# Three edits to the planner of a fused attention and SoLU kernel: the load time of chunk 3, the place of the centring of w_out, and q @ kv joined to the next chunk's kv

## The chip, the cores and the metric

The kernel runs on one core of one Trainium2 chip. The metric is the device time of one execution in microseconds (us). The kernel before took 196.27 us as the median of four runs, which lie between 195.92 and 196.62 us. Reading a profile, this text calls the engines by their short names: PE is TensorE (matrix products), ACT is ScalarE, DVE is VectorE, POOL is GpSimd, and SP is the engine that mostly issues stores here.

## What is computed

Two stages follow each other. The first is an attention without softmax for 8 batches and 8 heads of 576 positions and 64 channels, normed by its root mean square over the channels:

```python
kv = np.einsum('bhsd,bhse->bhde', k, v)
out = np.einsum('bhsd,bhde->bhse', q, kv)
rms = np.sqrt(np.mean(out * out, axis=-1, keepdims=True) + 1e-06)
x = out / rms * g_norm          # then heads side by side: 4608 tokens x 512
```

The second takes these 4608 rows through an expansion to 1024 channels, the SoLU activation (h times its softmax), a layer norm over the 1024 channels and a projection back to 512:

```python
h = x @ w_in
e = np.exp(h - h.max(-1)); sm = e / (e.sum(-1) + 1e-09)
solu = h * sm
ln = (solu - mean) / np.sqrt(var + 1e-06) * g_ln
out = ln @ w_out
```

Inputs and output are float32; the kernel computes its products in bf16.

## The kernel before

**Chunks.** The tokens are worked through in nine chunks of 512. Chunk c, for c from 0 to 7, holds the first 512 positions of batch c. Chunk 8 holds the last 64 positions of all batches. For a chunk the steps are: load k, v and q, which POOL issues as casting transfers (`load_kv`, L208, and `load_q`, L217); kᵀv of all heads (`kv_mm`, L275), 72 small products into one bank named misc and, from chunk 2 on, one bank named s; six copies of it to bf16 (`kv_copy`, L294, half of them on DVE and half on ACT from chunk 2 on); q turned so that channels lie on the partitions (`qT_mm` and `qT_copy` on PE for chunks 0 to 3, a transposing transfer of SP for the later ones); q @ kv for the first and the second half of the heads (`o_mm`, L337), each into two banks, mostly those named o; for each of these banks a square on ACT, a mean over the channels on PE (`s_mm`, into the single bank s), a logarithm and an exponential on ACT, and a product on DVE that makes x (`x_mul`, L387).

Then for each f of eight slices of 128 expanded channels: `h_mm` (L468, four products into one of two banks named h), an exponential on ACT (`h_exp`), the product u on DVE (`h_u`), the square of u on ACT or POOL (`u_sq`, called usq here), and for each pair of slices a sum of two exponentials on POOL (`e_sum`, called es). `sums` (L528) adds u, usq and es over the channels on PE into the bank misc (of chunk 0: into a bank h). `stats` on DVE and `rstd` on ACT turn these into one factor per token. `out_mm` (L581) is the projection, as two groups of four products for each of four blocks of 128 tokens, into one of two banks named out. `scale` (L612) multiplies a block by its factor on DVE, which frees the bank, and SP stores it.

The division by the sum of exponentials cancels in the layer norm, but for the constant that is added to the variance. The mean is taken out ahead of the projection: `w_mean` (L567) computes the weighted mean of the rows of w_out on PE into a bank out, and eight instructions of DVE, `w_center` (L575), write the centred, scaled bf16 weights that every `out_mm` reads. The bank of the mean is free again only after the last of them.

**The planner.** No order is written out. `Plan` (L19) gets pieces: a name, an engine, an assumed length, a rank, the pieces that it needs, and the buffers that it begins or uses. `order` (L33) is a greedy list scheduler. It keeps a clock for each engine and takes, again and again, the piece that can start earliest; where several could start at the same time, the one of the lowest rank. It models when buffers come free, a change of TensorE's tile shape (0.1 us, L67), and the load queue (L71 to L74): a load adds its assumed time to the queue, and its data count as there 1.3 us later. The order so found is the program order of each engine. On the chip each engine executes its own instructions in that order and waits where a piece is not ready, whatever else could run. The assumed times therefore take no time themselves; they only decide who stands behind whom.

Three products matter for tile shape: `kv_mm` and `o_mm` run in tiles of 64x64, `sums` in tiles of 128x32, everything else on the full 128x128.

Of the kernel before, what the change touches and what calls it, by code (L numbers as in the profile page):

```python
# [18 lines left out]
class Plan:  # L19
# [3 lines left out]


    def __init__(self, bufs):
        self.pieces, self.users, self.bufs = {}, {}, bufs

    def add(self, name, engine, length, rank, fn, needs=(), uses=(), first=(), load=0.0):
        self.pieces[name] = (engine, length, rank, fn, needs, first, load)
        for key in (*uses, *first):  # L30
            self.users.setdefault(key, []).append(name)

    def order(self):  # L33
        free, done, queue, lanes, mode = {}, {}, 2.5, [], {}
        held = {tag: [] for tag in self.bufs}
        waiting = {n: set(p[4]) for n, p in self.pieces.items()}
        behind = {}
        for n, needs in waiting.items():
            for m in needs:
                behind.setdefault(m, []).append(n)  # L40
        ready = [n for n, needs in waiting.items() if not needs]
        order = []
        while ready:
            best = None
            for n in ready:
                engine, length, rank, fn, needs, first, load = self.pieces[n]
                t = max([free.get(engine, 0.0)] + [done[m] for m in needs])
                more = {}
                for key in first:
                    old = held[key[0]] + more.setdefault(key[0], [])  # L50
                    more[key[0]].append(key)
                    if len(old) >= self.bufs[key[0]]:
                        last = self.users[old[-self.bufs[key[0]]]]
                        t = max([t] + [done.get(m, 1e9) for m in last])
                if load and len(lanes) >= 8:
                    t = max(t, lanes[-8])
                if t < 1e8 and (best is None or (t, rank) < best[:2]):
                    best = (t, rank, n)
            t, rank, n = best
            engine, length, rank, fn, needs, first, load = self.pieces[n]  # L60
            ready.remove(n)
            for key in first:
                held[key[0]].append(key)
            if engine == "pe":

                tiling = n[0] if n[0] in ("kv_mm", "o_mm", "sums") else "full"
                length += 0.1 if mode.get(engine, tiling) != tiling else 0.0  # L67
                mode[engine] = tiling
            free[engine] = t + length
            done[n] = t + length + {"pe": 0.2, "sp": 2.5}.get(engine, 0.12) + (2.0 if n[0] == "qT" and engine == "sp" else 1.0 if n[0] == "gate" else 0.0)  # L70
            if load:  # L71
                queue = max(queue, t + length + 1.0) + load
                done[n] = queue + 1.3
                lanes.append(done[n])  # L74
            order.append(fn)
            for m in behind.get(n, ()):
                waiting[m].discard(n)
                if not waiting[m]:
                    ready.append(m)
        assert len(order) == len(self.pieces)  # L80
        return order
# [3 lines left out]
def kernel(  # L85
# [21 lines left out]
    B, H, S, D = q.shape  # L107
# [5 lines left out]
    NC = B + 1  # L113
# [7 lines left out]
    bufs = {  # L121
        "k": 3, "v": 3, "q": 3, "qT": 3, "osq": 4, "lss": 2, "rst": 2, "oc": 2, "x": 2, "e": 4, "u": 2, "usq": 2, "es": 2,
        "ob": 4,
    }
# [8 lines left out]
    plan = Plan({**banks, **bufs})  # L133
# [113 lines left out]
    for b in range(B):  # L247
        at = b - 9.0 if b > 1 else (-2.0, -1.5)[b]
        behind = [] if b < 2 else [("h_mm", 0, 0)] if b == 2 else ([("gate", b - 1)] if b - 1 in XBAR else []) + [("h_mm", b - 3, 2 if b == 3 else 0)]
        for g, hs in enumerate(heads(b)):  # L250
            part = 0.1 * g
            n = len(heads(b))
            for i, (name, src) in enumerate((("k", k), ("v", v))):
                plan.add((name, b, g), "pool", 0.75 if n == 1 else 0.6, at + part + 0.01 * i,
                         lambda name=name, src=src, b=b, hs=hs: load_kv(name, src, b, hs),
                         behind, uses=[(name, b)] if g else [],
                         first=[] if g else [(name, b)], load=2.9 / n if b < 4 else 3.5)
            plan.add(("q", b, g), "pool", 0.9 if n == 1 else 0.7, at + part + (0.02 if b < 2 else 0.1),
                     lambda b=b, hs=hs: load_q(b, hs), behind,
                     uses=[("q", b)] if g else [], first=[] if g else [("q", b)], load=2.7 / n if b < 4 else 3.3)  # L260
        plan.add(("q_last", b), "pool", 0.6, 2.0 + 0.5 * b, lambda b=b: load_q_last(b),
                 [("h_mm", 2 + b // 2, 4 * (b % 2))], load=0.5)
    for half in range(2):
# [133 lines left out]
    for c in range(NC):  # L397
# [4 lines left out]
        if c < B:  # L402
            for xs in ((0,), (1,)) if c < 2 else ((0, 1),):
                g = xs[0]
                rg = r + 0.5 * w * g
                plan.add(("kv_mm", c, g), "pe", 0.65, rg, lambda c=c, xs=xs: kv_mm(c, xs), [("k", c, g), ("v", c, g)],
                         uses=[("k", c), ("v", c)], first=[(kv_tag(c, x), "kv", c, x) for x in xs])
                for x in xs:
                    for part in range(3):
                        plan.add(("kv", c, x, part), kv_engine(c, x), 0.25, rg + 0.05,  # L410
                                 lambda c=c, x=x, part=part: kv_copy(c, x, part), [("kv_mm", c, g)],
                                 uses=[(kv_tag(c, x), "kv", c, x)])
        if c in XBAR:
            plan.add(("qT", c), "sp", 1.8, r - 0.1, lambda c=c: q_turn(c),
                     [("q", c, 0)] if c < B else [("q_last", b) for b in range(B)],
                     uses=[("q", c)] if c < B else [], first=[("qT", c)])
# [3 lines left out]
        for hf in range(2):  # L420
            g = group(c, hf)
            tag = ("out", "h")[c] if c < 2 and hf else "o"
            if c not in XBAR:
# [7 lines left out]
                         first=[] if hf else [("qT", c)])  # L431
# [3 lines left out]
                     uses=[("qT", c)], first=[(tag, c, hf, z) for z in range(2)])  # L435
            for z in range(2):
                i = (c, hf, z)
                rz = r + w * (0.4 + 0.5 * hf + 0.12 * z)
                if (c, hf) in COPIED and z:
                    plan.add(("oc", i), "dve", 0.62, rz, lambda i=i: o_copy(*i), [("o_mm", c, hf)],  # L440
                             uses=[(tag, *i)], first=[("oc", i)])
                    plan.add(("sq", i), "pool", 1.05, rz + 0.01, lambda i=i: o_sq_copy(*i), [("oc", i)],
                             uses=[("oc", i)], first=[("osq", i)])
                else:
                    plan.add(("sq", i), "act", 0.57, rz, lambda i=i: o_sq(*i), [("o_mm", c, hf)],
                             uses=[(tag, *i)], first=[("osq", i)])
                stag = "h" if i in ((0, 0, 1), (0, 1, 0)) else "s"
                plan.add(("s_mm", i), "pe", 0.22, rz + 0.02, lambda i=i, stag=stag: s_mm(i, stag), [("sq", i)],
                         uses=[("osq", i)], first=[(stag, i)])
                if c == 0:  # L450
                    plan.add(("ex", i), "act", 0.6, rz + 0.04, lambda i=i: s_rsqrt(*i), [("s_mm", i)],
                             uses=[(stag, i)], first=[("rst", i)])
                else:
                    plan.add(("ln", i), "act", 0.6, rz + 0.03, lambda i=i: s_ln(*i), [("s_mm", i), "table"],
                             uses=[(stag, i)], first=[("lss", i)])
                    plan.add(("ex", i), "act", 0.6, rz + 0.04, lambda i=i: s_exp(*i), [("ln", i)],
                             uses=[("lss", i)], first=[("rst", i)])
                plan.add(("x", i), "dve", 0.67, rz + 0.06, lambda i=i: x_mul(*i),
                         [("ex", i)] + ([("x", (c, 0, 0))] if (hf, z) != (0, 0) else []),
                         uses=[(tag, *i), ("rst", i)] + ([("x", c)] if (hf, z) != (0, 0) else []),  # L460
                         first=[("x", c)] if (hf, z) == (0, 0) else [])
# [44 lines left out]
    for c in range(NC):  # L506
        for f in range(NF):
            r = c + f / 8
            plan.add(("h_mm", c, f), "pe", 0.87, r, lambda c=c, f=f: h_mm(c, f),
                     [("w_in", f // 4), *[("x", (c, *i)) for i in xs]], uses=[("x", c)], first=[(h_bank(c, f), "h", c, f)])  # L510
            plan.add(("exp", c, f), "act", 0.57, r + 0.02, lambda c=c, f=f: h_exp(c, f),
                     [("h_mm", c, f), "table"] + ([("exp", c, f - 1)] if f % 2 else []), uses=[(h_bank(c, f), "h", c, f)] + ([("e", c, f // 2)] if f % 2 else []),
                     first=[] if f % 2 else [("e", c, f // 2)])
            plan.add(("u", c, f), "dve", 0.62, r + 0.04, lambda c=c, f=f: h_u(c, f),
                     [("exp", c, f)] + ([("u", c, 0)] if f else []), uses=[(h_bank(c, f), "h", c, f), ("e", c, f // 2)] + ([("u", c)] if f else []),
                     first=[] if f else [("u", c)])
            engine = "act" if f in {0: (2, 4, 6, 7), 1: (), NC - 1: (1, 3, 5, 6, 7)}.get(c, (2, 6)) else "pool"
            plan.add(("usq", c, f), engine, 0.57 if engine == "act" else 1.05, r + 0.15 if c else -0.6,
                     lambda c=c, f=f, engine=engine: u_sq(c, f, engine), [("u", c, f)] + ([("usq", c, 0)] if f else []),
                     uses=[("u", c)] + ([("usq", c)] if f else []), first=[] if f else [("usq", c)])  # L520
            if f % 2:
                n = f // 2
                plan.add(("es", c, n), "pool", 1.28, r + 0.1, lambda c=c, n=n: e_sum(c, n),
                         [("exp", c, f)] + ([("es", c, 0)] if n else []), uses=[("e", c, n)] + ([("es", c)] if n else []),
                         first=[] if n else [("es", c)])
# [49 lines left out]
    def w_center(f):  # L575
        nc.vector.scalar_tensor_tensor(
            out=w_out_sb[:, f, :], in0=w_out_f[:, f, :].bitcast(FP32), scalar=g_ln_sb[:, f:f + 1],
            in1=T["mean"][:, :], op0=MUL, op1=SUB,
        )
# [48 lines left out]
    plan.add("w_mean", "pe", 2.0, -0.5, lambda: [w_mean(f) for f in range(NF)], ["w_out", "g_mean", ("o_mm", 0, 1)],  # L628
             first=[("out", "mean")])
    for f in range(NF):  # L630
        plan.add(("w_center", f), "dve", 0.67, 0.05 + 0.12 * f, lambda f=f: w_center(f), ["w_mean"], uses=[("out", "mean")])
    for c in range(NC):
        r, rs = (c + 1, c + 1) if c else (0.55, -0.5)
        parts = [[("u", c, f) for f in range(NF)], [("usq", c, f) for f in range(NF)], [("es", c, n) for n in range(NF // 2)]]
# [13 lines left out]
        for m in range(3 if c == NC - 1 else 4):  # L648
            tag = "o" if c == NC - 1 and m > 1 else "out"
            for half in range(2):  # L650
# [7 lines left out]
            plan.add(("store", c, m), "act" if c == NC - 1 and m % 2 else "sp", 0.6, r + (2 * m + 3) / 8, lambda c=c, m=m: store(c, m),  # L658
                     [("ob", c, m)], uses=[("ob", c, m)])

    for fn in plan.order():
        fn()

# [29 lines left out]
```

## Time and profile before

| | |
|---|---|
| median of four runs | 196.27 us (195.92 to 196.62) |
| profiled execution, its own time | 196.05 us |
| span of the profiled execution, first to last instruction | 194.3 us |
| mean granted TensorE clock | 0.994 |
| PE busy | 178.9 us (92%) |
| ACT busy | 140.2 us (72%) |
| POOL busy | 129.6 us (67%) |
| DVE busy | 122.2 us (63%) |
| DMA queue of the loads (software dynamic) | 17.30 MB, 54.8% of 16 engines' span |

The span is what the profile's rows lie in; the execution's own time is longer by what happens ahead of the first and behind the last instruction. A group of instructions in the timeline has its start, the time it covers, its engine, line and operation, the tiles written and read with their sizes, the number of instructions, and, in brackets, how long the engine stood idle before it and what ended that. Matmuls overlap, so the distance from one start to the next tells what one costs.

### The profile page before, as it was taken

Reading aid. Unit: us, or ns where it says so; the run is one execution under the profiler, and the core shown is the slowest. Engines: PE = TensorE matmul, PEld = TensorE weight load, DVE = VectorE, ACT = ScalarE, POOL = GpSimd, SP = SyncE. Lnnn points to the kernel's source line nnn. Section 1 sums busy time; section 2 is a strip of 40 time slices with the busy share of each in tenths; the row PEclk is TensorE's granted clock in tenths of the full one; section 3 lists DMA queues with packets and bytes.
Section 4 is the critical chain, followed back from the end, with each engine's and each line's share of the span. In section 5 each row is a group of like instructions: output and inputs, shape, how many; then the busy total and the mean of one; then the engine's idle time right before and its main releaser. Section 6 shows DMA issues by size and latency. Waiting matters only on the chain.

```text
span 194.3 us, 5441 instructions
## 1 busy us (share of the span) xinstructions
PE 178.9 (92%) x2282; PEld 88.4 (46%) x2282; DVE 122.2 (63%) x241; ACT 140.2 (72%) x244; POOL 129.6 (67%) x140
## 2 busy tenths in 40 slices
PE   7897998798699988999999999999999999999990
PEld 2342454453354443445436445445444554544560
DVE  1356578387866857749675965858594757665450
ACT  2028887979878897978879796988779496556420
POOL 7981799600789996897698977578385838846200
PEclk9999999999999999999999999999999999999997
DMA  2999999999995999999599994156111111211216
GB/s 34 200 203 279 343 203 204 203 208 272 230 203 79 164 202 209 173 198 201 148 173 223 219 185 134 59 113 174 54 54 57 57 54 57 108 57 54 110 22 198
DMA packets 36040, 29.71 MB, mean 153 GB/s; under 512 B 11816, under 2 KB 30512, under 8 KB 36016
## 3 DMA queue, kind: packets, MB, share of 16 engines
q0 software_dynamic: 20112, 17.30, 54.8%
q1 hardware_dynamic: 15616, 11.67, 20.8%
q10 hardware_dynamic: 288, 0.39, 0.6%
q8 instruction: 18, 0.29, 0.6%
q14 instruction: 6, 0.05, 0.1%
HBM read 32.51 MB, written 9.44 MB: 216 GB/s over the span
## 4 chain that ended last, share of the span: by engine, by line
PE 69%; DMA 15%; POOL 8%; ACT 3%; issue 2%; DVE 1%; POOLq 0%
PE out_ps L585 27%; PE h_ps L471 26%; DMA q_sb<-in_q_dram 11%; PE misc_ps L537 4%; DMA v_sb<-in_v_dram 4%; PE s_ps L369 3%; PE o_ps L348 3%; POOL usq_sb L497 2%; POOL k_sb L212 2%; POOL es_sb L503 1%; POOL v_sb L212 1%; PE misc_ps L286 1%; PE misc_ps L193 1%; PE h_ps L595 1%; PE o_ps L585 1%
## 5 line engine op out<-in xcount | busy, mean ns | idle before, releaser
L471 PE MATMUL h_ps<-x_sb,w_in_sb 128*128 128x512 bf16 x276 | 70.1, 380 | 1.1 <-DVE x_sb L390 1.1
L585 PE MATMUL out_ps<-w_out_sb,u_sb 128*128 128x512 bf16 x272 | 68.8, 380 | 1.4 <-DVE ob_sb L617 1.1
L497 POOL TENSOR_TENSOR usq_sb<-u_sb 128x512 bf16<-128x512 bf16 x51 | 52.9, 1045 | 21.5 <-DVE u_sb L486 21.4
L486 DVE TENSOR_TENSOR u_sb<-h_ps,e_sb 128x512 bf16<-128x512 f32 x69 | 47.3, 687 | 25.3 <-ACT e_sb L479 24.9
L503 POOL TENSOR_TENSOR es_sb<-e_sb 128x512 bf16<-128x512 f32 x36 | 45.8, 1273 | 23.5 <-ACT e_sb L479 23.4
L479 ACT ACTIVATE e_sb<-h_ps,zero_t 128x512 f32<-128x512 f32 x69 | 47.1, 682 | 13.4 <-PE h_ps L471 11.9
L471 PEld LDWEIGHTS <-w_in_sb 128*128 128x128 bf16 x288 | 27.2, 98 | 34.6 <-issue 4.0
L585 PEld LDWEIGHTS <-u_sb 128*128 128x128 bf16 x280 | 26.4, 98 | 33.0 <-issue 2.9
L390 DVE SCALAR_TENSOR_TENSOR x_sb<-o_ps,g_rep,rst_sb 128x512 bf16<-128x512 f32 x32 | 23.9, 750 | 11.0 <-ACT rst_sb L377 10.9
L617 DVE TENSOR_SCALAR ob_sb<-out_ps,rstd 128x512 f32<-128x512 f32 x33 | 24.5, 746 | 8.5 <-PE out_ps L585 4.4
L363 ACT ACTIVATE osq_sb<-o_ps,zero_t 128x512 bf16<-128x512 f32 x31 | 19.7, 682 | 12.8 <-PE o_ps L348 12.8
L377 ACT ACTIVATE rst_sb<-lss_sb,zero_t 128x512 f32<-128x512 f32 x32 | 23.3, 727 | 0.7
L373 ACT ACTIVATE lss_sb<-s_ps,eps_t 128x512 f32<-128x512 f32 x32 | 22.0, 688 | 2.2 <-PE s_ps L369 2.1
L495 ACT ACTIVATE usq_sb<-u_sb,zero_t 128x512 bf16<-128x512 bf16 x21 | 15.2, 722 | 6.1 <-DVE u_sb L486 6.0
L369 PE MATMUL s_ps<-osq_sb,head_mean 128*128 128x512 bf16 x34 | 12.9, 380 | 0.8 <-ACT lss_sb L373 0.4
L537 PEld LDWEIGHTS <-stat_sel 128*32 128x32 bf16 x720 | 10.1, 97 | 3.7 <-issue 3.2
L212 POOL DMA_DIRECT2D k_sb<-in_k_dram x10 | 7.9, 787 | 4.0 <-DMA w_in_sb<-in_moe_w_in_dram 2.6
L193 PE MATMUL s_ps<-zeros 128*128 128x512 bf16 x28 | 9.1, 447 | 1.4 <-DVE zero_t L158 1.2
L286 PE MATMUL misc_ps<-v_sb,k_sb 64*64 64x64 bf16 x360 | 7.6, 194 | 2.7 <-ACT lv L562 1.4
L286 PEld LDWEIGHTS <-k_sb 64*64 64x64 bf16 x576 | 6.7, 107 | 6.5 <-issue 6.5
L220 POOL DMA_DIRECT2D q_sb<-in_q_dram x10 | 8.6, 857 | 1.6 <-DMA w_in_sb<-in_moe_w_in_dram 1.4
L348 PE MATMUL o_ps<-qT_sb,kvd 64*64 64x32 bf16 (+1 forms) x240 | 8.1, 257 | 0.2 <-ACT qT_sb L321 0.2
(86 smaller groups left out, 131.9 us busy)
## 6 DMA issues: line engine op xcount, KB each, us to landing
out_dram<-ob_sb SPq DMA_DIRECT2D x34, 256.0 KB, 3.0
k_sb<-in_k_dram POOLq DMA_DIRECT2D x6, 576.0 KB, 12.7
v_sb<-in_v_dram POOLq DMA_DIRECT2D x6, 576.0 KB, 12.7
q_sb<-in_q_dram POOLq DMA_DIRECT2D x6, 512.0 KB, 14.6
w_out_f<-in_moe_w_out_dram POOLq DMA_DIRECT2D x1, 2048.0 KB, 16.2
k_sb<-in_k_dram POOLq DMA_DIRECT2D x4, 288.0 KB, 11.4
v_sb<-in_v_dram POOLq DMA_DIRECT2D x4, 288.0 KB, 12.1
q_sb<-in_q_dram POOLq DMA_DIRECT2D x4, 256.0 KB, 12.5
```

The costliest lines, as they stand in the source:

```text
L363: nc.scalar.activation(out=t[:, :], in_=T[("o", *i)].rearrange("p a b c -> p (a b c)"), func=AF.Square, bias=zero_t[:, :])
L369: nc.tensor.matmul(t[:, :], head_mean[:, :], T["osq", i][:, :], start=True, stop=True)
L373: nc.scalar.activation(out=t[:, :], in_=T["s", i][:, :], func=AF.Ln, bias=eps_t[:, :])
L377: nc.scalar.activation(out=t.rearrange("p a b c -> p (a b c)"), in_=T["lss", i][:, :], func=AF.Exp, scale=-0.5, bias=zero_t[:, :])
L390: nc.vector.scalar_tensor_tensor(out=T["x", c][:, 2 * hf:2 * hf + 2, z], in0=T["o", c, hf, z][:, :, :, :], scalar=g_rep[:, :], in1=T["rst" ...
L471: nc.tensor.matmul(t[:, :], w_in_sb[:, dt, f * 128:(f + 1) * 128], T["x", c][:, dt].rearrange("p a b c -> p (a b c)"), start=(dt == 0), st ...
L479: nc.scalar.activation(out=T["e", c, f // 2][:, f % 2, :], in_=T["h", c, f][:, :], func=AF.Exp, bias=zero_t[:, :])
L486: nc.vector.tensor_tensor(out=T["u", c][:, f, :], in0=T["h", c, f][:, :], in1=T["e", c, f // 2][:, f % 2, :], op=MUL)
L497: nc.gpsimd.tensor_tensor(out=dst, in0=src, in1=src, op=MUL)
L503: nc.gpsimd.tensor_tensor(out=T["es", c][:, n, :], in0=e[:, 0, :], in1=e[:, 1, :], op=ADD)
L585: nc.tensor.matmul(T["acc", c, m][:, :], T["u", c][:, f, m * 128:(m + 1) * 128], w_out_sb[:, f, :], start=(f == 0), stop=(f == NF - 1),)
L617: nc.vector.tensor_scalar_mul(out=t[:, :], in0=T["acc", c, m][:, :], scalar1=T["rstd", c][:, m:m + 1])
```

## The change

Four things are edited, in the planner and in what it is given.

1. In the load model, data of chunk 3 (k, v, q and its rest of q) count as there 5.3 us after their place in the queue where all others have 1.3 us. The assumed queue time of chunk 3's k and v becomes 3.5 us each (it was 2.9) and that of its q 3.3 us (it was 2.7), as for the later chunks.
2. Of the eight squares of u of chunk 0, ACT takes slices 1, 3, 5, 6 and 7, and POOL 0, 2 and 4. Before, ACT took 2, 4, 6 and 7, and POOL 0, 1, 3 and 5.
3. The rank of the eight centring instructions becomes 0.8 + 0.04 f; it was 0.05 + 0.12 f. The rank of u of chunk 0, slice f, is f/8 + 0.04, so that of the last, slice 7, is 0.915. It stood behind all eight centrings and is now behind three.
4. A new method `fuse` joins two pieces into one. It is used four times: the second half of q @ kv of chunks 3, 4, 5 and 6 with kᵀv of chunk 4, 5, 6 and 7. The joint piece has the rank of chunk number minus 0.9 (for chunk 4: 3.1). Alone, the second half of q @ kv has chunk number minus 0.75 (3.25), and kᵀv of the next chunk has chunk number minus 0.6 (3.4). It begins when everything that either part needs is there: two banks o, misc, s, and the data of the next chunk.

No instruction is added to the program or taken from it; one square of u moves from POOL to ACT, and the order of the others may change.

```diff
+    def fuse(self, names, rank):
+
+        parts = [self.pieces.pop(n) for n in names]
+        self.names.update({n: names[0] for n in names})
+        self.pieces[names[0]] = (
+            "pe", sum(p[1] for p in parts), rank, lambda: [p[3]() for p in parts], sum([list(p[4]) for p in parts], []),
+            sum([list(p[5]) for p in parts], []), 0.0,
+        )
+
     def order(self):
+        for n, p in self.pieces.items():
+            self.pieces[n] = (*p[:4], sorted({self.names.get(m, m) for m in p[4]} - {n}, key=str), *p[5:])
+        self.users = {key: sorted({self.names.get(m, m) for m in u}, key=str) for key, u in self.users.items()}
...
-                done[n] = queue + 1.3
+                done[n] = queue + (5.3 if n[1] == 3 else 1.3)
...
-                         first=[] if g else [(name, b)], load=2.9 / n if b < 4 else 3.5)
+                         first=[] if g else [(name, b)], load=2.9 / n if b < 3 else 3.5)
...
-                     uses=[("q", b)] if g else [], first=[] if g else [("q", b)], load=2.7 / n if b < 4 else 3.3)
+                     uses=[("q", b)] if g else [], first=[] if g else [("q", b)], load=2.7 / n if b < 3 else 3.3)
...
-            engine = "act" if f in {0: (2, 4, 6, 7), 1: (), NC - 1: (1, 3, 5, 6, 7)}.get(c, (2, 6)) else "pool"
+            engine = "act" if f in {0: (1, 3, 5, 6, 7), 1: (), NC - 1: (1, 3, 5, 6, 7)}.get(c, (2, 6)) else "pool"
...
-        plan.add(("w_center", f), "dve", 0.67, 0.05 + 0.12 * f, lambda f=f: w_center(f), ["w_mean"], uses=[("out", "mean")])
+        plan.add(("w_center", f), "dve", 0.67, 0.8 + 0.04 * f, lambda f=f: w_center(f), ["w_mean"], uses=[("out", "mean")])
...
+    for c in range(1, B - 3):
+        plan.fuse([("o_mm", c + 2, 1), ("kv_mm", c + 3, 0)], c + 1.1)
     for fn in plan.order():
         fn()
```

More of the change, by code (lines that the diff above doesn't have):

```diff
@@ L25, in __init__ @@
     def __init__(self, bufs):
-        self.pieces, self.users, self.bufs = {}, {}, bufs
+        self.pieces, self.users, self.bufs, self.names = {}, {}, bufs, {}
     def add(self, name, engine, length, rank, fn, needs=(), uses=(), first=(), load=0.0):
```

## The prediction

> **What bounds the kernel now.** I read the page first: busy times and the slices.
>
> ```profile
> PE 178.9 (92%) x2282; PEld 88.4 (46%) x2282; DVE 122.2 (63%) x241; ACT 140.2 (72%) x244; POOL 129.6 (67%) x140
> ...
> PE   7897998798699988999999999999999999999990
> ```
>
> One slice is 4.86 us. From slice 16 on (about 75 us) PE is full to the end, and the chain that ended last runs over PE without a gap there. So a microsecond saved on PE behind 75 us is one off the span, and so is one of PE's idle time ahead of it, if the rest keeps up. Idle are 194.3 - 178.9 = 15.4 us: some 3.8 before the first product of `h_mm` at full pace (19.5 us), 4.7 behind PE's last instruction (189.6 us), so 7.0 between 20 and 75 us. What ended them is in PE's waits:
>
> ```profile
> PE misc_ps L286 <- ACT lv L562: 1.4, 1, 1.4
> PE misc_ps L286 <- DMA v_sb<-in_v_dram: 1.2, 1, 1.2
> ...
> PE misc_ps L314 <- DMA q_sb<-in_q_dram: 1.1, 1, 1.1
> PE out_ps L585 <- DVE ob_sb L617: 1.1, 2, 1.0
> PE misc_ps L314 <- ACT kvd L306: 0.9, 1, 0.9
> ```
>
> L286 reads nothing that L562 writes, and its two banks had been freed by 37.7 us; so I take the first, before kᵀv of chunk 2, for v of chunk 2 landing near 38.9 us. The next two belong to chunk 3, in PE's timeline:
>
> ```profile
> 47.88 0.38 PE L369 MATMUL s_ps<-osq_sb,head_mean 128*128 128x512 bf16 x1
> 49.51 0.22 PE L286 MATMUL misc_ps<-v_sb,k_sb 64*64 64x64 bf16 x2 [1.25 <-DMA v_sb<-in_v_dram]
> ...
> 52.04 0.41 PE L348 MATMUL o_ps<-qT_sb,kvd 64*64 64x256 bf16 x8
> 53.57 0.62 PE L314 MATMUL misc_ps<-ident,q_sb 128*128 128x128 bf16 x8 [1.12 <-DMA q_sb<-in_q_dram]
> ```
>
> Behind both stand groups of `h_mm` of chunk 1 that need no load. The loads can't come sooner: the page's row of DMA is at nine tenths or more in every slice from 5 to 58 us, and a q issued at 31.4 us lands at 53.5. DVE's timeline shows the centring ahead of u of slice 7:
>
> ```profile
> 27.29 5.35 DVE L576 SCALAR_TENSOR_TENSOR w_out_sb<-w_out_f,g_ln_sb,out_ps 128x512 bf16<-128x512 f32 x8
> 32.55 0.68 DVE L486 TENSOR_TENSOR u_sb<-h_ps,e_sb 128x512 bf16<-128x512 f32 x1
> ```
>
> The tile shapes show in starts. First a half of q @ kv alone (chunk 4), then kᵀv of chunk 4 beside q @ kv of chunk 3, adjacent already:
>
> ```profile
> 82.04 1.03 PE L471 MATMUL h_ps<-x_sb,w_in_sb 128*128 128x512 bf16 x4
> 82.99 0.41 PE L348 MATMUL o_ps<-qT_sb,kvd 64*64 64x256 bf16 x8
> 83.34 1.04 PE L585 MATMUL out_ps<-w_out_sb,u_sb 128*128 128x512 bf16 x4
> ...
> 65.33 1.03 PE L585 MATMUL out_ps<-w_out_sb,u_sb 128*128 128x512 bf16 x4
> 66.29 0.22 PE L286 MATMUL misc_ps<-v_sb,k_sb 64*64 64x64 bf16 x2
> ...
> 66.88 0.42 PE L348 MATMUL o_ps<-qT_sb,kvd 64*64 64x256 bf16 x8
> 67.23 1.04 PE L471 MATMUL h_ps<-x_sb,w_in_sb 128*128 128x512 bf16 x4
> ```
>
> **What the Trainium skill says.** TensorEngine Tiling (Array Packing), Key Properties: changing the tiling mode drains TensorE. The trace agrees: four products of 512 columns take 0.864 us start to start, but 0.95 ahead of q @ kv. ScalarE: Activation LUTs, What ACT_TABLE_LOAD costs: an activation with pointer bias takes about 280 ns + 0.833 ns a column, back-to-back ones overlapping by some 93 ns: 0.71 us for 512, 0.61 in a row. The trace has 0.72 for a square of u. DMA: Bandwidth & Descriptors, Issuing engines are not separate DMA queues: all transfers end on the same 16 engines. It fits: issuing chunk 3 sooner would not land it sooner.
>
> **The change, part by part.**
>
> *Centring and squares of chunk 0.* The exponential of slice 7 ends at 28.74. With three centrings ahead (27.29 + 2.0 = 29.3) u of slice 7 ends near 30.0 where it ended at 33.2; its square runs on ACT at 30.0 (it ran at 33.27). POOL loses one square, 1.05 us, so its last sum of exponentials, which ended at 34.9, ends near 33.9; the loads of chunks 3 and 4 that it issues in between move by as much and gain nothing, as their queue is full (v of chunk 4 took 22.9 us to land). `sums` of chunk 0 (36.25 to 37.5) can then go at about 34.4: 1.9 us sooner. It holds one of the two h banks that the second half of q @ kv of chunk 1 needs; that ran at 39.49, behind the bank and behind kᵀv of chunk 2. It can now run near 37.3, ahead of the landing at 38.9. Against that: centrings 4 to 8 come one u (0.65 us) later. The first projection waits some 0.6 us at 30.05, the one that needs the mean's bank (0.26 us of wait at 32.69) some 0.5; turning q's first half on ACT waits up to 0.5 behind the square; and ACT gets one square more, 0.72 us, into gaps of 0.76 and 0.69 us that it has at 26.7 and 29.5. PE's work between is the same. Up to `h_mm` of chunk 1 (46.16 us) it has, counted from 38.65, kᵀv 0.6, four groups of the projection 3.5, two turns of q 0.9, q @ kv 0.35 and three means 0.6: 6.0, so 44.7. Gain 1.5; I take 1.2 for the queued copies on ACT. Bounds: -0.6 (the delayed projection only) to 2.2 (all of the 39.49 to 37.3).
>
> *Loads of chunk 3 planned late.* The queue model now puts v of chunk 3 at about 43.1 + 3.5 + 5.3 = 51.9 us and q at 55.2, where they landed at 49.5 and 53.5. Both pieces move behind work that is ready, so 1.25 + 1.12 = 2.37 us of waiting can go. Not all of it does: the third group of `h_mm` of chunk 1 needs the bank that u frees at 49.2, so without kᵀv PE still stands from 48.26 to 49.2, 0.95 us, and some 0.4 more for the next bank. That leaves 1.0. Cover: nothing reads kᵀv of chunk 3 before 60.23, where its q @ kv waits for banks o anyway; it would have to come 8 us later to hold that up. The three copies of ACT (0.81 us, at 50.4) move too and let two exponentials forward. Bounds: 0 to 2.4.
>
> *Joining.* Apart, kᵀv of chunk 5 costs 88.30 - 86.63 - 0.864 = 0.81 us and q @ kv 83.34 - 82.04 - 0.864 = 0.44: 1.25. Together (chunk 3 with 4) they cost 67.23 - 65.33 - 0.864 = 1.04. So 0.21 for a pair, for three pairs 0.6, less 0.1 as q @ kv of chunk 6 stands behind `sums` already: 0.5; the first is adjacent already: 0. What may be late next is `sums`: it needs misc, which kᵀv now fills before it, until DVE has made its copies (0.89 us). Of chunk 2 it ran at 84.31; joined work at 82.99 and a group behind it put it at 84.95, 0.65 us later. From its end over `stats`, ACT and the scaling to a free out bank took 85.54 to 88.86, and the projection used that bank at 89.17: 0.3 us of slack, and kᵀv, 0.8 us of what PE did meanwhile, is gone from there. I charge 0.4 in all, since groups of `h_mm` can fill most; net 0.1. Bounds: -4.1 (rival below) to 0.5. The data are in time: v of chunk 5 was issued at 63.4, at the median of 12.7 us it lands at 76.1, and the joint piece can't start before 82.4, when banks o are free.
>
> *Sum:* 1.2 + 1.0 + 0.1 = 2.3 us. 194.3 - 2.3 = 192.0 of span; the profiled execution's own 196.05 becomes 193.75. The median of the runs shown lies 0.22 above it: 194.0.
>
> **Rivals.** A change within 0.3%, 0.6 us, is not told from none here.
>
> *ACT caps it (0.20).* From 40 to 50 us ACT is busy 9.29 of 10. If it has no room, only the square that moved to 30 us, 0.7 us, and a little of the chunk 3 waits are won: about 1.0, so 195.3. For it: that row. Against: ACT has 1.16 us idle at 54, behind PE's wait for q.
>
> *Stalls move only (0.10).* PE waits as long on banks as it did on loads, and the joining is eaten by the later `sums`: 196.2. Against: at 53.6 the projection of chunk 1 has its first four slices of u, ready as filler.
>
> *The out bank decides (0.14), slower.* At the adjacent pair of before, chunks 3 and 4, `sums` comes straight behind (68.29 us), ACT works off copies and squares, and PE then waits 0.41 us on s and 0.96 on an out bank. If the joining makes that pattern in three more chunks, it costs 3 x 1.37 = 4.1, against 0.5 + 2.2: 196.27 + 1.4 = 197.7. It decides once the three pairs lose over 0.9 us each.
>
> *All gaps close (0.10).* PE's idle time in 20 to 75 us falls to about 2.5: 4.5 + 0.5 gained, 191.3.
>
> **How the numbers follow.** My forecast has 0.46, with a range of its own of 193.0 to 195.0. Faster by over 0.3% are forecast, closed gaps and most of the ACT case: 0.75. Same: stalls that move and the rest of the ACT case: 0.11. Slower: 0.14. A range of 191.6 to 196.7 leaves out half of the closed gaps and most of the slower case, under 2 in 10.
>
> **What would show it.** u of chunk 0, slice 7, near 29.3; `sums` of chunk 0 near 34.5; q @ kv of chunk 1 ahead of kᵀv of chunk 2; `h_mm` of chunk 1 near 45. No wait of PE on v or q of chunk 3; kᵀv of chunk 3 behind 50 us. Four adjacent pairs of some 1.04 us. Wrong would be: PE waits on L617, L373 or L304 that add up behind 75 us, or `h_mm` of chunk 1 still at 46.

## The result

The changed kernel is as fast as the one before: the ratio of its runs to those of before, taken on the same chips, is 0.9999, with a 95% interval from 0.9981 to 1.0017. The forecast was 194.0 us, 2.3 us faster. The ratio leaves out the 15 slowest of its 36 runs, so the median of all of them, 197.58 us against 196.08 before, tells another side: 21 of the 36 were granted a mean TensorE clock of 0.991 or less and took 196.55 to 200.45 us, where no run of before whose clock is on record was granted less than 0.993.

The profiled execution took 195.96 us at a mean clock of 0.998, with a span of 194.2 us (before: 196.05 and 194.3). Busy times and PE's slices on the page after:

```profile
PE 179.8 (93%) x2282; PEld 89.5 (46%) x2282; DVE 122.2 (63%) x241; ACT 140.8 (73%) x245; POOL 128.3 (66%) x139
...
PE   7799896989799999999969999999999999999990
```

Of the 40 slices of 4.86 us, the 15th and 16th (68 to 78 us) are full now, where they had an 8; but the 21st (97 to 102 us) has a 6, where the kernel before had a 9. PE's waits name it:

```profile
PE misc_ps L550 <- POOL usq_sb L510: 1.8, 1, 1.8
PE misc_ps L299 <- DMA v_sb<-in_v_dram: 1.7, 2, 1.2
...
PE h_ps L484 <- DVE u_sb L499: 0.9, 1, 0.9
PE misc_ps L327 <- ACT kvd L319: 0.9, 1, 0.9
```

(Lines after the planner have moved by 13: L550 is `sums`, L537 before; L510 is the square, L497 before; L299 is `kv_mm`; L348 is `load_gate`, L335 before.) The two waits on v are those of chunks 0 and 2. No wait on v or q of chunk 3 and none on an out bank is left. What is new is one wait of 1.83 us in `sums` of chunk 3, on PE's timeline after:

```profile
97.17 0.63 PE L550 MATMUL misc_ps<-u_sb,stat_sel 128*32 128x128 bf16 x32
97.63 0.56 PE L550 MATMUL misc_ps<-usq_sb,stat_sel 128*32 128x128 bf16 x28
100.02 0.24 PE L550 MATMUL misc_ps<-usq_sb,stat_sel 128*32 128x128 bf16 x4 [1.83 <-POOL usq_sb L510]
100.07 0.41 PE L550 MATMUL misc_ps<-es_sb,stat_sel 128*32 128x128 bf16 x16
```

28 of the 32 products on squares ran; the last four need the square of slice 7. It is late on POOL, whose timeline after says why:

```profile
93.71 1.27 POOL L516 TENSOR_TENSOR es_sb<-e_sb 128x512 bf16<-128x512 f32 x1
98.80 0.18 POOL L348 COPY landed<-q_sb 1x1 bf16<-1x1 bf16 x1 [3.82 <-DMA q_sb<-in_q_dram]
98.94 1.03 POOL L510 TENSOR_TENSOR usq_sb<-u_sb 128x512 bf16<-128x512 bf16 x1
```

The copy at 98.80 is `load_gate` of chunk 6. It copies one element of q, so that nothing behind it on POOL starts before that q has landed; the planner has it there to hold the loads of the next chunk back. POOL stands 3.82 us before it, and the square stands behind it.

In the kernel before, the same copy waited too, but `sums` of chunk 3 came at 102.03 us, long after the square behind the copy (95.96 us) was done. POOL and then PE before:

```profile
95.83 0.18 POOL L335 COPY landed<-q_sb 1x1 bf16<-1x1 bf16 x1 [1.84 <-DMA q_sb<-in_q_dram]
...
98.18 0.83 POOL L212 DMA_DIRECT2D k_sb<-in_k_dram  x1
```

```profile
102.03 0.63 PE L537 MATMUL misc_ps<-u_sb,stat_sel 128*32 128x128 bf16 x32
102.49 0.62 PE L537 MATMUL misc_ps<-usq_sb,stat_sel 128*32 128x128 bf16 x32
```

So two things crossed. `sums` of chunk 3 moved from 102.03 to 97.17. And q of chunk 6 landed 3 us later, at 98.8 instead of 95.8: the k of chunk 5 was issued at 65.38 instead of 62.59, that of chunk 6, behind the copy for chunk 5, at 82.79 instead of 79.67.

The books of the two profiled executions can be closed with one more number. The first k and v of the run after landed late: the first kᵀv began at 8.75 us (7.71 before), and full pace of chunk 0's `h_mm` at 20.30 (19.50), ahead of anything that was edited. The last group of products begins at 187.65 (187.70). So 0.05 + 0.8 for the start + 1.83 for the new wait = 2.7 us had been gained elsewhere, as far as two executions tell. (The late start is no work of the edits: a run of the kernel before with nothing but two copies moved, `before_gates` below, began at 8.82 and 20.35.)

### The profile page after: what moved, and what is told of

The parts are those of the page before. It is cut to its first block, busy times and chain, and to the rows that moved or that the text cites. A ratio compares the mean times of both kernels' runs of the same rounds, so it can differ in the third digit from the quotient of the medians.

```text
span 194.2 us, 5442 instructions
## 1 busy us (share of the span) xinstructions
PE 179.8 (93%) x2282; PEld 89.5 (46%) x2282; DVE 122.2 (63%) x241; ACT 140.8 (73%) x245; POOL 128.3 (66%) x139
## 4 chain that ended last, share of the span: by engine, by line
PE 62%; DMA 19%; POOL 7%; ACT 5%; DVE 3%; issue 2%; POOLq 0%
PE out_ps L598 25%; PE h_ps L484 22%; DMA v_sb<-in_v_dram 11%; DMA q_sb<-in_q_dram 7%; PE misc_ps L550 3%; POOL usq_sb L510 3%; PE s_ps L382 3%; PE o_ps L361 3%; ACT e_sb L492 2%; POOL k_sb L225 2%; DVE u_sb L499 1%; PE misc_ps L299 1%; DVE x_sb L403 1%; ACT lss_sb L386 1%; ACT rst_sb L390 1%
## 5 line engine op out<-in xcount | busy, mean ns | idle before, releaser
L510 POOL TENSOR_TENSOR usq_sb<-u_sb 128x512 bf16<-128x512 bf16 x50 | 51.7, 1041 | 21.9 <-DVE u_sb L499 21.8
L508 ACT ACTIVATE usq_sb<-u_sb,zero_t 128x512 bf16<-128x512 bf16 x22 | 15.8, 719 | 6.2 <-DVE u_sb L499 6.2
L550 PEld LDWEIGHTS <-stat_sel 128*32 128x32 bf16 x720 | 10.2, 97 | 5.9 <-issue 5.8
L206 PE MATMUL s_ps<-zeros 128*128 128x512 bf16 x28 | 9.8, 478 | 1.4 <-DVE zero_t L171 1.2
L299 PE MATMUL misc_ps<-v_sb,k_sb 64*64 64x64 bf16 x360 | 7.8, 194 | 1.7 <-DMA v_sb<-in_v_dram 1.7
L317 DVE CAST kvd<-misc_ps 64x128 bf16<-64x128 f32 (+1 forms) x24 | 6.9, 288 | 3.7 <-PE misc_ps L299 2.7
```

The costliest lines, as they stand in the source:

```text
L510: nc.gpsimd.tensor_tensor(out=dst, in0=src, in1=src, op=MUL)
```

## The experiments

Theory 1: the edits do gain some 2 us, and lose it at one place, where the copy that waits for a load stands ahead of a square that TensorE needs. Theory 2: there is no gain to free; if that wait goes, another comes. A third suspicion was the joining, since it holds TensorE, two banks and data together.

**The copy behind the square.** Of the changed kernel, one need of one piece:

```diff
-                plan.add(("gate", c), "pool", 0.15, r - 12.0, lambda c=c: load_gate(c), [("q", c, 0)], uses=[("q", c)])
+                plan.add(("gate", c), "pool", 0.15, r - 12.0, lambda c=c: load_gate(c), [("q", c, 0)] + ([("usq", 3, 7)] if c == 6 else []), uses=[("q", c)])
```

> The changed kernel, with the tiny copy of POOL that waits for q of chunk 6 placed behind the square of u of chunk 3, slice 7, instead of ahead of it. Theory 1 (the gate: that square stands behind the copy on POOL, so TensorE's sums of chunk 3 wait for a load): the 1.8 us wait of TensorE on the square goes, 194.2 to 194.7 us, under 0.995 of before; the loads of chunk 7 go out some 2 us later and land in time. Theory 2 (the gain never was there, the late start of sums is only where it shows): the wait goes and another of like size comes ahead of 134 us, 195.7 to 196.3.

It took 193.35 us against 196.14: 0.9865 (0.9839 to 0.9891). POOL's and PE's timelines of this run:

```profile
94.94 1.03 POOL L510 TENSOR_TENSOR usq_sb<-u_sb 128x512 bf16<-128x512 bf16 x1
95.92 0.57 POOL L239 DMA_DIRECT2D q_last<-in_q_dram  x1
99.29 0.18 POOL L348 COPY landed<-q_sb 1x1 bf16<-1x1 bf16 x1 [2.80 <-DMA q_sb<-in_q_dram]
```

```profile
96.83 0.63 PE L550 MATMUL misc_ps<-u_sb,stat_sel 128*32 128x128 bf16 x32
97.29 0.62 PE L550 MATMUL misc_ps<-usq_sb,stat_sel 128*32 128x128 bf16 x32
97.73 0.40 PE L550 MATMUL misc_ps<-es_sb,stat_sel 128*32 128x128 bf16 x16
```

POOL still waits 2.80 us for the same q, which lands even later, at 99.3. But the square is done, and PE goes through. It gained more than expected, 1.35% where theory 1 had some 0.9%, and it beats both kernels. The traces, which both reach full pace of `h_mm` at 20.3 us, are 2.19 us apart at the last group of products (185.46 against 187.65), so the wait of 1.83 is most of it. Part of the rest are the changed kernel's runs at a low clock, six of which are in its ratio; none of the six runs here was granted less than 0.994.

**The queue times of chunk 3 as before.** Was it that chunk 5's loads went out later?

```diff
-                         ... load=2.9 / n if b < 3 else 3.5)
+                         ... load=2.9 / n if b < 4 else 3.5)
...
-                     ... load=2.7 / n if b < 3 else 3.3)
+                     ... load=2.7 / n if b < 4 else 3.3)
```

> The changed kernel with the assumed queue times of chunk 3's k, v and q as before (2.9 and 2.7), while they still count as there 5.3 us behind it. The planner then puts the gate of chunk 4 and the loads of chunk 5 ahead by some 1.5 to 2 us on POOL, and all later loads with them. Theory 1 (loads issued late reach the gate late): q of chunk 6 lands 1.4 us or more sooner, the wait of TensorE on the square shrinks from 1.8 to 0.4 us or less, 194.6 to 195.0. Theory 2 (no gain there to free): 195.7 to 196.3.

It took 197.85 us against 196.14: 1.0100 (1.0064 to 1.0137), slower, so both expectations missed by the median. Three of the six runs were granted a clock of 0.990 or 0.991 and took 198.2 to 198.8 us; the profiled one, at 0.999, took 196.15, so its trace doesn't hold the whole 1.0100. The loads did go out sooner (k of chunk 6 at 81.07) and q of chunk 6 landed at 97.7. But with the queue planned shorter, the planner put the copy for chunk 5 ahead of a square as well. `sums` of chunks 2 and 3 on PE:

```profile
80.62 0.24 PE L550 MATMUL misc_ps<-usq_sb,stat_sel 128*32 128x128 bf16 x4 [1.03 <-POOL usq_sb L510]
...
100.19 0.24 PE L550 MATMUL misc_ps<-usq_sb,stat_sel 128*32 128x128 bf16 x4 [1.62 <-POOL usq_sb L510]
```

Two waits of the same make, 2.6 us. That 1.62 of 1.83 us are left with a q that lands 1.1 us sooner doesn't show that the landing decides little, since POOL's order changed here too: a sum of two exponentials stands between the copy and the square.

```profile
97.74 0.18 POOL L348 COPY landed<-q_sb 1x1 bf16<-1x1 bf16 x1 [4.58 <-DMA q_sb<-in_q_dram]
97.88 1.26 POOL L516 TENSOR_TENSOR es_sb<-e_sb 128x512 bf16<-128x512 f32 x1
99.11 1.03 POOL L510 TENSOR_TENSOR usq_sb<-u_sb 128x512 bf16<-128x512 bf16 x1
```

With the square straight behind the copy, 1.23 us sooner, some 0.4 us of the wait would be left by these lines (an estimate), which is what theory 1 expected. So how much of the wait is the late landing of q stays open.

**The same with both copies behind their squares.** The queue times are those of the run above; the need is new.

```diff
...
-                plan.add(("gate", c), "pool", 0.15, r - 12.0, lambda c=c: load_gate(c), [("q", c, 0)], uses=[("q", c)])
+                plan.add(("gate", c), "pool", 0.15, r - 12.0, lambda c=c: load_gate(c), [("q", c, 0)] + ([("usq", c - 3, 7)] if c > 4 else []), uses=[("q", c)])
```

> The changed kernel with the queue times of chunk 3 as before, and with the copies of POOL that wait for q of chunks 5 and 6 each placed behind the square of slice 7 of u that sums of chunk 2 and 3 need. In the run with the queue times alone, the copy for chunk 5 had come ahead of such a square too, and TensorE waited on squares 2.6 us in two places. Theory 1 (the place of the copy): no wait of TensorE on squares, 193.0 to 194.0 us, 3 to 4 us under the run without this. Theory 2 (the smaller queue times themselves cost): 195.5 or more.

193.52 us against 196.17: 0.9862 (0.9845 to 0.9878), 4.3 us under the run without it. No wait of PE on a square is left. The profiled executions, 193.60 us against 196.15, differ by 2.55 us, about the length of the two waits (2.65); the rest of the 4.3 lies in the other run's later executions, three of them at a low clock. That is the place of the copy again, with another load model.

**TensorE's side of the crossing.** POOL's order is left as it is up to the loads behind the copy, and `sums` of chunk 3 comes two groups of products later.

```diff
-        plan.add(("sums", c), "pe", 1.2, rs + 0.1, ...
+        plan.add(("sums", c), "pe", 1.2, rs + (0.27 if c == 3 else 0.1), ...
```

> The changed kernel, POOL's order untouched, with the rank of sums of chunk 3 raised by 0.17, so that two groups of products, 1.7 us, come ahead of it on TensorE. Theory 1 (TensorE stands at that place because its next instruction waits on POOL, which waits for q of chunk 6): POOL still waits 3 to 4 us for q, TensorE at sums 0 to 0.6 us, 193.4 to 194.8. If the delay on POOL itself is what costs, wherever TensorE stands: 195.7 to 196.3.

193.51 us against 196.24: 0.9876 (0.9848 to 0.9904). POOL waits for q as in the changed kernel, and PE does not wait:

```profile
97.97 0.18 POOL L348 COPY landed<-q_sb 1x1 bf16<-1x1 bf16 x1 [3.84 <-DMA q_sb<-in_q_dram]
98.10 1.03 POOL L510 TENSOR_TENSOR usq_sb<-u_sb 128x512 bf16<-128x512 bf16 x1
```

```profile
98.90 0.63 PE L550 MATMUL misc_ps<-u_sb,stat_sel 128*32 128x128 bf16 x32
99.36 0.62 PE L550 MATMUL misc_ps<-usq_sb,stat_sel 128*32 128x128 bf16 x32
```

So 3.84 us of idle POOL cost nothing by themselves that can be told from none (0.9876 here, 0.9865 with the copy moved). They cost when TensorE's next instruction is one that needs what stands behind them.

**No copy for chunk 6 at all.**

```diff
-        behind = ... ([("gate", b - 1)] if b - 1 in XBAR else []) + ...
+        behind = ... ([("gate", b - 1)] if b - 1 in XBAR and b < 7 else []) + ...
...
-            if c < B - 1:
+            if c < B - 2:
```

> The changed kernel without the copy of POOL that waits for q of chunk 6; the loads of chunk 7 then go out when POOL reaches them. Takes the wait away where the earlier run moved it. Theory 1: the 1.8 us go as they did there, 193.0 to 193.9 us. If it were the place of other POOL work that had helped there, and not the wait for the load: 195.5 to 196.3.

197.85 us against 196.17: 1.0056 (1.0035 to 1.0078). Thirteen of the 22 runs, the profiled one among them, were granted 0.989 or less; the other nine took 196.00 to 196.90 us, so the 193.0 to 193.9 of theory 1 missed in these too. The wait on the square went, as theory 1 said, and another came in its place. PE's timeline, and SP's transposing transfers of chunks 6 and 7:

```profile
112.22 0.64 PE L361 MATMUL o_ps<-qT_sb,kvd 64*64 64x256 bf16 x8 [2.59 <-DMA qT_sb<-q_sb]
```

```profile
97.92 6.79 SPq L341 DMA_TRANSPOSE qT_sb<-q_sb  x1
...
109.96 3.82 SPq L341 DMA_TRANSPOSE qT_sb<-q_sb  x1
```

POOL now issues the loads of chunk 7 at 95 to 97 us, just ahead of the transposing transfer of chunk 6. That takes SP 6.79 us where it took 2.06 in the changed kernel, and its data land 14.3 us after its issue where they took 6.1; q @ kv of chunk 6 waits for them at 112.22. Why the two disturb each other was not tried further, and it rests on this one trace. So the copy's wait has a use, and the expectation, which saw only its cost, failed.

**Which edit is worth what.** First, parts of the changed kernel with the copy where it was. Without the joining (the two lines with `fuse` at the end taken out):

> The changed kernel without the four joint pieces. Theory 1 (the gate): the order on POOL around the loads is nearly that of the changed kernel, the gate still ahead of the square, so the wait of TensorE on the square of chunk 3 stays at 1 us or more: 195.8 to 196.6. Rival (the joining brought sums of chunk 3 forward and loads back, and is what costs): no such wait, 194.8 to 195.4.

196.07 us against 196.14: 0.9972 (0.9951 to 0.9992). PE's waits on the square, from an execution of 198.62 us:

```profile
PE misc_ps L550 <- POOL usq_sb L510: 2.6, 1, 2.6
```

So the wait stays without any joint piece, as theory 1 said, and the joining isn't its cause. That the same kernel took 0.9894 with the copy moved (below) says that the crossing cost it too. Without edit 1 (its three lines as before):

> The changed kernel with the load model of before; centring and joining stay. Theory 1: the loads of chunks 5 to 7 go out as in the kernel before or sooner, no wait of TensorE on squares above 0.3 us, but the two waits for v and q of chunk 3 are back, together 1.5 to 2.4 us: 195.5 to 196.1. Rival (the joining costs): a wait on squares stays and the load waits come on top: 196.5 to 197.5.

196.46 us: 1.0025 (1.0004 to 1.0046). It is above the 195.5 to 196.1 us of theory 1; the twelve of its 22 runs that were granted 0.994 or more have a median of 196.03, within it, and the ten at 0.990 or less, the profiled one (197.64) among them, took 197.14 to 198.57. No wait on squares is left, but PE waits for v of chunk 3 longer than in the kernel before, 2.68 us, as v landed about 1.1 us later and PE came to it 0.35 us sooner; and a wait for an out bank follows:

```profile
PE misc_ps L299 <- DMA v_sb<-in_v_dram: 4.2, 4, 2.7
PE out_ps L598 <- issue: 1.3, 8, 0.2
PE s_ps L206 <- DVE zero_t L171: 1.2, 1, 1.2
PE out_ps L598 <- DVE ob_sb L630: 1.2, 1, 1.2
```

Then the parts with the copies moved, so that the crossing hides nothing. Without the joining, copy for chunk 6 behind its square:

> The changed kernel without the joint pieces, with the copy for chunk 6 behind the square of u of chunk 3, slice 7. Against the same kernel with them (193.35 us) it tells what joining is worth once the wait for the load is gone. The forecast's step has a saving of 0.2 us for each of three pairs and something taken back behind sums: 193.4 to 194.0. If the joining takes back more than it saves: under 193.3.

194.18 us against 196.17: 0.9894 (0.9878 to 0.9911), a little above what was expected: the joining is worth more than I had put it at. Without edits 2 and 3 (the squares' slices and the rank of the centring as before), both copies moved:

> The changed kernel with centring and squares of chunk 0 as before, and with the copies for chunks 5 and 6 behind the squares that sums of chunks 2 and 3 need. Against the changed kernel with the copy moved (193.35 us) it tells what the centring is worth. The forecast's step has 1.2 us: 194.2 to 194.9. If the earlier sums of chunk 0 gain nothing: 193.0 to 193.7.

193.89 us: 0.9886 (0.9871 to 0.9902), between the two expectations. Edit 1 alone on the kernel before, both copies moved:

> Edit 1 alone (chunk 3's loads planned late) on the kernel before, with the copies for chunks 5 and 6 behind those squares. From the runs so far, joining and centring are worth about 0.5 us each with the copy moved, so edit 1 should give the rest: 1.7 us, 194.2 to 194.8. The forecast's step had 1.0 for it: 195.0 to 195.4. If it only works together with the others: 195.7 or more.

194.52 us against 196.24: 0.9917 (0.9892 to 0.9943), as expected. And as a control the kernel before with both copies moved:

> The kernel before, with the copies of POOL for q of chunks 5 and 6 behind the squares of slice 7 of u of chunks 2 and 3, as in the runs that were fast. A control. If the three edits bring the gain and the copy's place only lets it through: no gain here, 195.6 to 196.9, since TensorE waits on no square in this kernel. If the place of the copy alone is worth the gain: 193.3 to 194.3.

195.95 us: 0.9988 (0.9974 to 1.0001). No gain that can be told from none: the place of the copies lets the gain through, and the edits bring it.

| with the copies moved | ratio to before | 95% interval |
|---|---|---|
| the kernel before | 0.9988 | 0.9974 to 1.0001 |
| edit 1 alone | 0.9917 | 0.9892 to 0.9943 |
| all but the joining | 0.9894 | 0.9878 to 0.9911 |
| all but squares and centring | 0.9886 | 0.9871 to 0.9902 |
| all | 0.9865 | 0.9839 to 0.9891 |
| all, queue times of chunk 3 as before | 0.9862 | 0.9845 to 0.9878 |

In the rows "all" and "all but the joining" only the copy for chunk 6 was moved, as the one for chunk 5 stood behind its square already. The rows without the joining and without squares and centring were measured on the same chip as the last row, so I set them against its 0.9862, although it differs from "all" in the queue times: without the joining 0.32% or 0.6 us are lost, without squares and centring 0.24% or 0.5 us; the intervals of both differences reach close to none, and set against the row "all" they include no difference. Edit 1 alone is 0.83%, 1.6 us. They add up to 2.7 us, which is what all have, but two of these are losses when one edit is left out and one is a gain of an edit alone, so the sum proves no independence. Edit 1 is worth more beside the others: without it, the other two are not faster than the kernel before (copies where they were; with them moved this was not run).

## Why the prediction was wrong

**The failed step.** "Loads of chunk 3 planned late" saw in edit 1 only two pieces of PE that come later. Of POOL the prediction said only, in the step on the centring, that loads of chunks 3 and 4 move and gain nothing; nowhere did it follow POOL's order past them, and so it put the cost there at nothing. `load_gate` is not in it, though it stood in the view that it read: POOL idle before L335 for 2.5 us in the kernel before, 1.84 of it at 95.83. The question that the step on the joining asked, whether the data of chunk 5 are in time, was put to the one that reads them on PE (76.1 us against 82.4: in time), and not to what stands behind the copy that waits for them. What the runs showed in its place: the copy for chunk 6 holds POOL for 3.82 us and, behind it, a square that PE needs, for which PE stands 1.83 us; with the square ahead of the copy (193.35 us) or `sums` behind both (193.51) the gain is there.

**The order of `sums`.** The step on the joining placed the joint piece at 82.99 us and `sums` of chunk 2 behind it at 84.95, later than before. It was the other way: `sums` came at 79.41, ahead of the joint piece at 84.41, and that of chunk 3 at 97.17, 4.9 us sooner than before. I had taken the order around the joint piece from the kernel before, and not from what the edits upstream did to it. It is edit 1 that moved `sums`: in every trace with it, or with its 5.3 us alone, `sums` of chunk 3 starts at 96.35 to 97.55 us (98.90 where it was put later by hand), without the joining too (96.94), and in the three without edit 1 at 99.27 to 103.49. That u of a chunk was planned to be done sooner is my reading of this, and not shown. That also emptied the slower rival: no wait on an out bank came up behind 75 us. The rival that stalls only move (0.10) had the right time for the wrong reason. It expected waits on banks and a later `sums`; it was an earlier `sums`, and a wait on POOL.

**Terms that were mis-sized.** With the copy moved, the sum of 2.3 us stands against 2.8 measured (193.35 against 196.14; by the ratio 2.6). That the sum comes so near is luck: one term was more than twice too large, the other two too small.

- Squares and centring: 1.2 in the forecast, about 0.5 measured. What it said of the order came: u of slice 7 at 29.96, `sums` of chunk 0 at 34.71, q @ kv of chunk 1 at 37.86, ahead of kᵀv of chunk 2, all in a run that began 0.8 us late. But `h_mm` of chunk 1 began at 46.49, 0.5 sooner if the late start is taken off, and near the 46 that the prediction had named as a sign of being wrong. Its count of PE's work from 38.65 us, ahead of its own landing of v at 38.9, had some 0.25 us too much in it. Two groups of the projection stood ahead of the first mean of chunk 1's second half on PE, and ACT waited 1.19 us for it.
- Loads of chunk 3: 1.0 in the forecast, 1.6 alone and, beside the others, 0.9865 against 1.0025, so 3.1, of which some 0.4 is the low clock of the runs without it (median 196.46, against 196.03 of those at 0.994 or more). No wait for chunk 3's data is left, and PE stood 0.90 us for the next bank, where the step had 0.95; kᵀv ran at 55.05. It had counted what two waits last in the kernel before. The wait for v isn't a fixed length: it was 2.68 us in the run without edit 1.
- Joining: 0.1 in the forecast, after 0.4 taken back behind `sums`; about 0.6 measured. The pair costs 85.39 - 83.45 - 0.864 = 1.08 us (1.04 in the step), and nothing was taken back.

**What was right.** The bound: PE behind 75 us, and its idle time before that. The cap by ACT, for which the prediction had 195.3 us, did not show: with the copy moved the kernel took 193.35, PE's full stretch begins sooner, and ACT's busy time rose by the one square only, from 140.2 to 140.8.

**Left open.** Why the transposing transfer takes three times as long beside the loads of the next chunk was not tried. Nor was how far the landing of q of chunk 6 varies from run to run; in the traces where the copy waited for it, it came between 95.4 and 99.7 us. None of the changed kernel's runs at a low clock has a trace, so where its clock fell isn't shown.

## What to carry over

When an edit moves a piece in a planned order, follow every in-order queue that the planner also fills, and list each instruction there that waits for a transfer and what stands behind it; a wait on an idle engine is free until the bound engine comes to need what is queued behind it. An edit upstream is itself such a change: pieces far behind it can be planned sooner, as `sums` was here, and meet waits that had been covered. And a wait that costs may still have a use: put it behind the work that is needed, before taking it away. A wait of the bound engine can also cost more than its length, as the last section shows.

## What was not expected of the hardware

A long wait of TensorE was followed by a stretch at half clock. In the run without the joining PE stood 2.63 us for the square, until 100.59 us; the page's rows of PE and its granted clock have this in the 21st and 22nd slice (98 to 108 us):

```profile
PE   7798896997999999999859999999999999999990
...
PEclk9999999999999999999978999999999999999999
```

Taken in steps of a quarter of a microsecond, the clock is 0.50 from 101.2 to 104.6 us and 1.00 on both sides. Groups of `h_mm` that take 0.864 us take 1.70 there, so the stretch costs some 1.7 us on top of the wait. The same comes behind the two other long waits: 2.68 us for v in the run without edit 1 (0.50 from 51.9 to 55.4), and 2.59 us for the transposed q in the run without the copy for chunk 6 (0.50 from 112.2 to 115.6). In the other ten traces no wait of PE is longer than 1.83 us, and its clock stays at 1.00 until its work is done. One such stretch lowers the mean clock of an execution by about 0.009 (an estimate: 1.7 us of 196). Of the 53 executions of the seven kernels here whose longest wait is 1.51 us or less, none was granted less than 0.993, while the changed kernel (longest wait in its trace 1.83 us) was granted 0.991 or less in 21 of 36. That a later q lengthens the wait in those until the clock falls fits all this, but it isn't shown. Its other 15 executions have a median of 195.59 us.

A transposing transfer of chunk 6's q took SP 2.06 us, and landed 6.1 us after its issue, with the loads of the next chunk held back; it took 6.79 us and landed after 14.3 with them issued 1 to 3 us ahead of it. Three loads of one chunk, issued within 1.6 us, landed one behind the other: k of chunk 6 7.6 us after its issue at 82.79, v 10.4 and q 14.3.
